# All sums of weights by the middle of the third up projection, and banks 2 and 3 of the scores in one visit for the first pair of each batch too

## The chip, the core and the metric

The kernel runs on one core of one Trainium2 chip. The metric is the device time of one execution in microseconds (us), lower is better. PE is TensorE (matmuls), DVE VectorE, ACT ScalarE, POOL GpSimd, SP SyncE, which here only starts DMAs.

## What is computed

Windowed causal attention over 8 batches, 8 heads, 576 positions and 64 dimensions per head, and then, on the attention's output taken as 4608 tokens of 512 features, a bilinear feed-forward: two up projections to 1536 features, multiplied element by element, and one down projection.

```python
scores = (q @ k.transpose(0, 1, 3, 2)) / sqrt(64) + slope[h] * (-abs(rel))    # rel = query - key
attn   = softmax(where((rel >= 0) & (rel < 128), scores, -1e9))
x      = (attn @ v).transpose(0, 2, 1, 3).reshape(8 * 576, 512)
out    = ((x @ w_a) * (x @ w_b)) @ w_out                                       # float32 in and out
```

## The kernel before, in words

**Numbers.** Almost every matmul operand is held as two float16 halves, high and low, and a product is three matmuls (high·high, high·low, low·high). `terms` (the matmul at line L820) does that for one stored form of weights against one stored form of activations: 2 blocks of the inner dimension by 3, so 6 matmuls of 128 rows by 288 columns.

**Batches and stages.** The program goes through the batches one after the other. For batch b there is an up stage ("up b" below, twelve units, one per block f of 128 hidden features) and a down stage ("down b", 48 steps of six matmuls, L916). The attention of a later batch runs in between their steps: beside up b run the third and fourth pair of heads of batch b+1, beside down b the first and second pair of batch b+2. Batch 0 is handled by code of its own (`first_attention`, `first_up`, `first_down`).

**Two kinds of up unit.** `up_plain` makes the two halves of the tokens by both projections, 4 steps of 12 matmuls: 48 matmuls. It reads the forms 0 to 3 of the block's weights. `up_fast` gets the same by seven products of sums and differences, 7 steps of 6 matmuls: 42 matmuls. It needs the activations' sums (`split_x`, on POOL, ACT and DVE, done one stage earlier) and the weights' sums (forms 3 to 6 of `wup`). Two lanes of fast units, even and odd f, are interleaved on PE. Beside its matmuls a fast unit gives ACT three reads of PSUM and a cast, DVE four adds or products and the low half of the result, and POOL one product of 128x288 elements (L875), whose result the unit's end needs.

**Sums of weights.** `sums_of_weights(f)` makes them in two steps per f, 24 steps for the twelve f. One step ("a sum" below) is five additions on POOL (L239 to L243), a cast on ACT (L244) and a subtraction on DVE (L245). Its two work tiles `wa` and `ws` come from the tag "t" with four buffers, which go round in the order of the code and which the scores use too, so POOL may have to wait at L239 or L240 until DVE has normalized an older bank of scores (L384). A sum writes over form 3, which a plain unit reads, so it can only follow the plain unit of its block. `quota` says how many sums are woven into which steps of the up and down stages 1, 2, 3; `ways` says which units of a batch are plain and which fast.

**The attention's visits.** `attention` is a generator of seven visits per pair of heads. It makes four banks of scores in PSUM: banks 0 and 1 first, later 2 and 3. A bank is some matmuls (L366), then DVE adds the bias and takes the row minimum (L370), ACT exponentiates (L371); `normalize` divides two banks at a time (ACT L383, DVE L384) into `phl`, which one DMA transposes into `pT` (L389) when all four are done. In the middle visit `pv` of the pair before runs: 42 small matmuls (L485) into two PSUM tiles `x_ps`. Score banks and `x_ps` share three PSUM buffers (`ps_at`), so the next score bank behind `pv` needs the buffer of bank 2, which is free when DVE has read bank 2. For the pairs p = 1 and p = 3 bank 3 stands behind bank 2 in the same visit; for p = 0 it stands one visit later, and p = 0 always lies in a down stage.

**What sets the order.** In the batches from 1 on PE follows the code's order exactly (`manual_schedule`); on DVE, ACT, POOL and SP a list scheduler picks the order from its own estimates at build time, and the reads of PSUM in the fast units carry a high priority. On the chip each engine's queue runs strictly in its order and waits on semaphores.

The lines that the change's two parts turn on:

```python
ways = [(every, [])] * 2 + [(every[6:], every[:6])] + [([], every)] * (B - 3)        # (plain, fast) of each batch
# per batch: ((first step, last step, sums) in the up stage, the same in the down stage)
quota = [((), ()), (((8, 48, 6),), ((0, 48, 4),)), (((0, 24, 2), (28, 66, 3)), ((0, 48, 3),)), (((0, 48, 6),), ())] + ...
# attention, middle visit of a pair (bank 2, then the product with v of the pair before)
scores(o, 2); pv(prev.p, st, prev, prev.vhl)
if two == 2 and p in (1, 3): scores(o, 3)            # otherwise one visit later
```

Of the kernel before, what the change touches and what calls it, by code (L numbers as in the profile page):

```python
# [21 lines left out]
B, H, S, D = 8, 8, 576, 64  # L22
# [24 lines left out]
def attention_then_bilinear_ffn(ctx: ExitStack, tc: tile.TileContext, qT, kT, vP, w_a, w_b, w_out, rel, slopes2, outT):  # L47
# [204 lines left out]
    def load_v(b):  # L252

        st = State()
        st.v = work.tile([P, NPAIR, VCOLS], F32, tag="v", name="v")
        sp.dma_start(st.v, vP[b])
        st.xq = work.tile([P, S], BF16, tag="xq", name="xq")
        return st
# [44 lines left out]
    def qk_squares(b, p, qk):  # L303
        o = State()
        o.b, o.p, o.qk = b, p, qk
        sums = small.tile([P, 1], F32, tag="qs", name="qs")
        hi = work.tile([P, 2, S], F16, tag="qkh", name="qkh", bufs=2)
        lo = work.tile([P, 2, S], F16, tag="qkl", name="qkl", bufs=2)
        act.activation(lo.bitcast(BF16), qk, AF.Square, accum_out=sums)

        o.both = small.tile([P, 2], BF16, tag="both", name="both")
        vec.tensor_scalar(out=o.both, in0=halves, scalar1=sums, scalar2=None, op0=ALU.mult)
        o.kh, o.kl = hi, lo
        return o
# [103 lines left out]
    def split(n, src):  # L418
        act.copy(xs[:, n, 0, :, :], src)  # L419
        vec.tensor_tensor(out=xs[:, n, 1, :, :], in0=src, in1=xs[:, n, 0, :, :], op=ALU.subtract)  # L420

    def split_x(st, plain, fast):

        b11, b12, b21, b22 = (st.v[:, k:k + 2, t:t + HT] for k in (0, 2) for t in (0, HT))
        split(0, b11)
        if plain:
            split(1, b21)
            split(2, b22)
            split(B12, b12)
        if not fast:  # L430
            return
        yield
        pool.tensor_tensor(out=b11, in0=b12, in1=b11, op=ALU.subtract)
        if not plain:
            split(2, b22)
        pool.tensor_tensor(out=b12, in0=b22, in1=b12, op=ALU.subtract)
        split(4, b11)
        pool.tensor_tensor(out=b22, in0=b22, in1=b11, op=ALU.subtract)
        yield
        if not plain:  # L440
            split(1, b21)
        split(6, b12)
        pool.tensor_tensor(out=b21, in0=b21, in1=b22, op=ALU.subtract)
        yield
        split(5, b22)
        split(3, b21)
        yield
# [194 lines left out]
    def attention():  # L642


        n = NPAIR * (B - 1)
        qks = {}

        def load(i):
            if i < n:

                qks[i] = (load_plain_qk if i < NPAIR else load_qk)(1 + i // NPAIR, i % NPAIR)

        def squares(i):
            if i >= n:
                return None
            qk = qks.pop(i)
            return qk if i < NPAIR else qk_squares(1 + i // NPAIR, i % NPAIR, qk)

        def split(o):
            if o and o.b > 1:  # L660
                split_qk(o)

        def lay_out(o):
            if o:
                before_scores(o, lay_out_qk(o) if o.b > 1 else -8.0)

        def behind():

            return tc.issue_after(last_read[0].ins) if last_read[0] else ExitStack()

        load(0)
        st, prev = load_v(1), None
        o = squares(0)
        lay_out(o)
        load(1)
        yield 0
        for i in range(n + 1):
            b, p = 1 + i // NPAIR, i % NPAIR

            two = 2 if o and o.b >= 2 else 1  # L680
            for bi in range(two if o else 0):
                scores(o, bi)
            with behind():
                nxt = squares(i + 1)
            if p == 1 and b > 1:
                st = load_v(b)
            if p == 2:
                v_scale(st)
            yield i + 1 / 7
            if o and two == 1:  # L690
                scores(o, 1)

            if p == 2:

                with tc.issue_after(first_reads[0].ins) if first_reads[0] else ExitStack():
                    late.vhl = split_v(st, late.p)
            elif prev and p != 1:
                prev.vhl = split_v(st, prev.p)
            yield i + 2 / 7
            if p == 2:  # L700
                pv(late.p, st, late, late.vhl)
                transpose_probs(prev)
                split(nxt)
            if o and p != 2:
                with behind():
                    normalize(o)
            if p != 2:
                split(nxt)
            yield i + 3 / 7
            if o:  # L710
                scores(o, 2)
            if prev and p not in (1, 2):
                pv(prev.p, st, prev, prev.vhl)
            if two == 2 and p in (1, 3):
                if p == 2:
                    with behind():
                        normalize(o)
                scores(o, 3)
            yield i + 4 / 7
            if p == 2:  # L720
                prev.vhl = split_v(st, prev.p)
                if two == 1 or p not in (1, 3):
                    with behind():
                        normalize(o)
            if o and (two == 1 or p not in (1, 3)):
                scores(o, 3)
            lay_out(nxt)
            load(i + 2)
            if p == 1:
                v_squares(st, (0, 1))  # L730
            if prev and p == 0:
                states[b - 1] = st
                assert started["down"] == b - 2
                for k, _ in enumerate(split_x(st, b - 1 <= 2, b - 1 >= 2)):
                    yield i + (4.2 + 0.2 * k) / 7
            yield i + 5 / 7
            if o:
                with behind():
                    normalize(o)
            if p == 1:  # L740
                v_squares(st, (2, 3))
            yield i + 6 / 7
            if prev and p == 0:
                hidden_scale(st)
            if p == 2:
                pv(prev.p, st, prev, prev.vhl)
            if p == 1:
                late = prev
            elif o:
                transpose_probs(o)  # L750
            prev, o = o, nxt
            yield i + 1
# [221 lines left out]


    every = list(range(NF))
    ways = [(every, [])] * 2 + [(every[6:], every[:6])] + [([], every)] * (B - 3)
    att = Pace(attention())
    spread = chain.from_iterable(sums_of_weights(f) for f in every)

    quota = [((), ()), (((8, 48, 6),), ((0, 48, 4),)), (((0, 24, 2), (28, 66, 3)), ((0, 48, 3),)), (((0, 48, 6),), ())] + [((), ())] * (B - 4)

    def first_batch():
        st = states[0]
# [60 lines left out]
```

## Time and profile before

| | |
|---|---|
| time, median of 3 runs | 1011.96 us (1011.73 to 1013.79) |
| the profiled execution | 1013.37 us, of which the traced span is 1011.6 us |
| PE busy | 969.4 us, 96% of the span |
| DVE, ACT, POOL busy | 681.8, 643.0, 305.9 us |
| PE's share of the chain of waits | 60%, DVE 12%, ACT 6%, DMA 6% |
| up 1 (all plain, 6 sums) | 81.56 us |
| down 1 (4 sums) | 42.00 us |
| up 2 (6 plain and 6 fast, 5 sums) | 80.79 us |
| down 2 (3 sums) | 41.48 us |
| up 3 (all fast, 6 sums) | 76.40 us |

How to read it: the stages' times are the distances between the first up or down matmul of one stage and that of the next, on PE's row of the timeline. A row of the stretches view gives start and end, the length, the busy time of each engine in it with the number of its instructions, the clock that TensorE was granted (1.00 is full), the share of the DMA engines and what they moved. A row of the waits view gives who waited for whom, the total in us, how often and the longest. A timeline row gives start, length, engine, line, operation, shapes and count, and in brackets the idle time before it with what ended it.

### The profile page before, as it was taken

To read this page: it belongs to the slowest core of one execution; us is meant where nothing else is said; L and a number is where in the kernel's file an instruction comes from. 1 tells how busy PE (TensorE), PEld (TensorE's weight loads), DVE (VectorE), ACT (ScalarE), POOL (GpSimd) and SP (SyncE) were. 2 spreads that over 40 slices of the span, in tenths; PEclk is the share of its full clock that TensorE was granted. 3 is DMA by queue.
4 is the path that set the end of the run, shared out by engine and by line. 5 is a ranking of instruction groups with operands and counts; after the bars stand their busy time and mean duration, and the time that the engine had idled before them with its cause. 6 is when DMAs were issued, how large, how long until landed. Compare 5 with 4: busy or idle time off the path is not lost.

```text
span 1011.6 us, 23876 instructions
## 1 busy us (share of the span) xinstructions
PE 969.4 (96%) x9327; PEld 753.2 (74%) x9327; DVE 681.8 (67%) x1884; ACT 643.0 (64%) x1668; POOL 305.9 (30%) x347
## 2 busy tenths in 40 slices
PE   8789889999999999999899999999999999999998
PEld 6557666777777777776687777777777778777776
DVE  5988999567767666787776577766677576434430
ACT  6976779666666657667666776667667766423321
POOL 3533463001445313464724022221223022221100
PEclk9889999999999999999999999999999999999999
DMA  9307643574346242464424642464423632210001
GB/s 344 132 33 276 222 124 68 113 189 87 68 96 164 67 89 57 92 161 104 87 49 107 171 89 43 95 171 101 90 63 95 168 67 43 49 36 7 1 13 36
DMA packets 148433, 102.83 MB, mean 102 GB/s; under 512 B 120032, under 2 KB 128352, under 8 KB 147296
## 3 DMA queue, kind: packets, MB, share of 16 engines
q1 hardware_dynamic: 138816, 91.77, 37.0%
q10 hardware_dynamic: 9504, 9.54, 2.9%
q8 instruction: 73, 1.20, 0.5%
q14 instruction: 40, 0.33, 0.1%
HBM read 48.33 MB, written 9.44 MB: 57 GB/s over the span
## 4 chain that ended last, share of the span: by engine, by line
PE 60%; DVE 12%; DMA 6%; ACT 6%; issue 2%; POOL 2%; SPq 0%; ACTq 0%; DVEq 0%; POOLq 0%
PE ch L820 16%; PE dn_ps L916 16%; PE p L820 12%; PE up_ps L820 11%; PE x_ps L485 3%; DMA v<-in_vP 3%; DVE phl L384 3%; PE sc_ps L366 2%; ACT t L371 2%; DVE xs L420 1%; DMA qk<-in_kT 1%; DVE t L370 1%; ACT phl L383 1%; POOL wup L135 1%; DMA qst<-qkl 1%
## 5 line engine op out<-in xcount | busy, mean ns | idle before, releaser
L820 PEld LDWEIGHTS <-wup 128*128 128x128 f16 x4212 | 407.8, 98 | 126.7 <-issue 20.5
L916 PE MATMUL dn_ps<-h,wdn 128*128 128x288 f16 x2016 | 254.0, 286 | 0.1
L820 PE MATMUL ch<-xs,wup 128*128 128x288 f16 x1584 | 228.2, 286 | 7.1 <-DVE rc L880 4.2
L916 PEld LDWEIGHTS <-wdn 128*128 128x128 f16 x2016 | 193.9, 98 | 52.1 <-issue 0.3
L820 PE MATMUL up_ps<-xs,wup 128*128 128x288 f16 x1440 | 184.8, 288 | 6.2 <-DVE rc L769 4.6
L820 PE MATMUL p<-xs,wup 128*128 128x288 f16 x1188 | 178.0, 286 | 1.1 <-ACT rc L863 1.1
L875 POOL TENSOR_TENSOR rc<-rc,row 128x288 f32<-128x288 f32 x66 | 63.8, 966 | 241.2 <-DVE row L873 223.7
L371 ACT ACTIVATE t<-t,mn 128x192 f32<-128x192 f32 (+2 forms) x252 | 107.1, 427 | 33.3 <-DVE mn L370 33.2
L384 DVE SCALAR_TENSOR_TENSOR phl<-t,rin,phl 128x192 f16<-128x192 f32 (+2 forms) x252 | 104.6, 451 | 29.1 <-ACT phl L383 28.8
L813 ACT CAST h<-rc 128x576 f16<-128x576 f32 x96 | 64.2, 669 | 64.6 <-DVE rc L880 31.9
L383 ACT ACTIVATE phl<-t,rin 128x192 f16<-128x192 f32 (+2 forms) x252 | 88.5, 426 | 16.4 <-DMA pT<-phl 10.9
L814 DVE TENSOR_TENSOR h<-rc,h 128x576 f16<-128x576 f32 x90 | 73.4, 815 | 28.8 <-ACT h L813 28.2
L370 DVE CUSTOM_DVE_ANT_0 t<-sc_ps,bias,neg 128x192 f32<-128x192 f32 (+2 forms) x216 | 73.7, 390 | 8.6 <-PE sc_ps L366 8.6
L420 DVE TENSOR_TENSOR xs<-v,xs 128x576 f16<-128x576 f32 x51 | 52.1, 1032 | 28.6 <-ACT xs L419 28.1
L857 ACT ACTIVATE row<-ch,g 128x288 f32<-128x288 f32 x66 | 32.9, 498 | 58.1 <-PE ch L820 58.1
L135 POOL TENSOR_TENSOR wup<-wup,wdn 128x512 int32<-128x512 int32 x36 | 54.6, 1537 | 44.2 <-DVE wup L133 14.1
L921 ACT ACTIVATE row<-dn_ps,oi 128x288 f32<-128x288 f32 x56 | 27.8, 496 | 60.5 <-PE dn_ps L916 59.9
L852 DVE TENSOR_TENSOR rc<-p,rc 128x288 f32<-128x288 f32 x66 | 30.0, 454 | 44.9 <-PE p L820 34.8
L239 POOL TENSOR_TENSOR wa<-wup 128x512 f32<-128x512 f16 x24 | 30.5, 1270 | 64.8 <-DVE phl L384 40.2
L348 POOL TENSOR_SCALAR bias<-rel_sb,ninv,sl_sb 128x192 f32<-128x192 f32 x24 | 18.0, 751 | 102.6 <-DVE mn L370 96.8
L880 DVE SCALAR_TENSOR_TENSOR rc<-rc,g,ch 128x288 f32<-128x288 f32 x66 | 33.6, 509 | 22.6 <-PE ch L820 22.5
L414 POOL TENSOR_TENSOR xq<-xq,sq 128x576 bf16<-128x576 bf16 x22 | 31.3, 1424 | 54.8 <-ACT sq L413 54.4
(143 smaller groups left out, 1334.0 us busy)
## 6 DMA issues: line engine op xcount, KB each, us to landing
v<-in_vP SPq DMA_DIRECT2D x8, 1280.0 KB, 6.9
out<-row ACTq DMA_DIRECT2D x60, 144.0 KB, 2.0
qk<-in_qT SPq DMA_DIRECT2D x28, 288.0 KB, 3.9
qk<-in_kT SPq DMA_DIRECT2D x28, 288.0 KB, 4.4
wdn<-in_w_a SPq DMA_DIRECT2D x12, 512.0 KB, 4.5
wdn<-in_w_b SPq DMA_DIRECT2D x12, 512.0 KB, 5.4
wdn<-in_w_out SPq DMA_DIRECT2D x12, 512.0 KB, 4.4
qst<-qkh SPq DMA_DIRECT2D x24, 144.0 KB, 2.5
```

The costliest lines, as they stand in the source:

```text
L135: pool.tensor_tensor(out=t[:, m, :], in0=t[:, m, :], in1=low[:, m, :], op=ALU.add)
L370: vec.tensor_tensor_reduce(out=t[:, c:c + w], in0=ps[:, c:c + w], in1=o.bias[:, WIN - w:WIN], scale=-0.125 if o.b == 1 else o.neg, scalar= ...
L371: act.activation(t[:, c:c + w], t[:, c:c + w], AF.Exp, bias=o.mn[:, n:n + 1], scale=-1.0, accum_out=o.sm[:, n:n + 1])
L383: act.activation(phl[:, 0, pc:pc + w], e, AF.Copy, scale=s)
L384: vec.scalar_tensor_tensor(out=phl[:, 1, pc:pc + w], in0=e, scalar=s, in1=phl[:, 0, pc:pc + w], op0=ALU.mult, op1=ALU.subtract)
L420: vec.tensor_tensor(out=xs[:, n, 1, :, :], in0=src, in1=xs[:, n, 0, :, :], op=ALU.subtract)
L813: act.copy(h[:, f, :, 0, :], hid)
L814: eng.tensor_tensor(out=h[:, f, :, 1, :], in0=hid, in1=h[:, f, :, 0, :], op=ALU.subtract)
L820: pe.matmul(ps[:, 0:HT], wup[:, a[0], a[1], wi, k, :], xs[:, b, xi, k, :], start=(first and n == 0), stop=(last and n == len(ks) - 1), ski ...
L875: pool.tensor_tensor(out=x0, in0=x0, in1=mid, op=ALU.mult)
L880: vec.scalar_tensor_tensor(out=x1, in0=x1, scalar=st.g, in1=ch, op0=ALU.mult, op1=ALU.mult)
L916: pe.matmul(ps[:, 0:HT], wdn[:, f, wi, e * P:(e + 1) * P], h[:, f, t, hi, :], start=(m == 0 and n == 0), stop=(m == NF - 1 and n == 2))
```

## The change

Two independent things. First, batch 2 loses its six plain units: all twelve are fast. So that the sums are there in time, eleven of the 24 are woven into up 1 (six before), six into down 1 (four), seven into the first 60 of the 84 steps of up 2 (five into 66), and none into down 2 and up 3 (three and six). `split_x` no longer makes the form of the activations that only plain units read (slot `B12`) for batch 2. Second, the first pair of each batch (p = 0, from batch 2 on) gets bank 3 in the middle visit, right behind `pv`, as p = 1 and p = 3 do.

```diff
-            if two == 2 and p in (1, 3):
+            if two == 2 and p in (0, 1, 3):
...
                 scores(o, 3)
             yield i + 4 / 7
             if p == 2:
                 prev.vhl = split_v(st, prev.p)
-                if two == 1 or p not in (1, 3):
+                if two == 1 or p not in (0, 1, 3):
                     with behind():
                         normalize(o)
-            if o and (two == 1 or p not in (1, 3)):
+            if o and (two == 1 or p not in (0, 1, 3)):
                 scores(o, 3)
...
-                for k, _ in enumerate(split_x(st, b - 1 <= 2, b - 1 >= 2)):
+                for k, _ in enumerate(split_x(st, b - 1 < 2, b - 1 >= 2)):
...
-    ways = [(every, [])] * 2 + [(every[6:], every[:6])] + [([], every)] * (B - 3)
+    ways = [(every, [])] * 2 + [([], every)] * (B - 2)
...
-    quota = [((), ()), (((8, 48, 6),), ((0, 48, 4),)), (((0, 24, 2), (28, 66, 3)), ((0, 48, 3),)), (((0, 48, 6),), ())] + [((), ())] * (B - 4)
+    quota = [((), ()), (((5, 48, 11),), ((0, 48, 6),)), (((0, 60, 7),), ())] + [((), ())] + [((), ())] * (B - 4)
```

PE's queue gets 72 rows shorter, 36 matmuls and their 36 loads of weights: 288 `up_ps` rows go, 144 `ch` and 108 `p` rows come.

On POOL at the start of up 2, where `wa` and `ws` are a sum's tiles and L875 is a fast unit's product, there stood before (first the end of the plain units, with L875 of the first fast unit in the last row):

```order
L239 TENSOR_TENSOR wa_5332<-wup 128x512
L348 TENSOR_SCALAR bias<-rel_sb,ninv,sl_sb 128x192
L240 TENSOR_TENSOR ws_5333<-wa_5332 128x128
L241 TENSOR_TENSOR ws_5333<-wa_5332 128x128
L242 TENSOR_TENSOR ws_5333<-ws_5333,wa_5332 128x128
L243 TENSOR_TENSOR ws_5333<-wa_5332,ws_5333 128x128
L414 TENSOR_TENSOR xq<-xq,sq 128x576
L875 TENSOR_TENSOR rc<-rc,row 128x288
```

At the start of up 2 POOL now has this:

```order
L239 TENSOR_TENSOR wa_5118<-wup 128x512
L240 TENSOR_TENSOR ws_5119<-wa_5118 128x128
L241 TENSOR_TENSOR ws_5119<-wa_5118 128x128
L875 TENSOR_TENSOR rc<-rc,row 128x288
L242 TENSOR_TENSOR ws_5119<-ws_5119,wa_5118 128x128
L243 TENSOR_TENSOR ws_5119<-wa_5118,ws_5119 128x128
L875 TENSOR_TENSOR rc<-rc,row 128x288 x2
L348 TENSOR_SCALAR bias<-rel_sb,ninv,sl_sb 128x192
L239 TENSOR_TENSOR wa_5255<-wup 128x512
L240 TENSOR_TENSOR ws_5256<-wa_5255 128x128
L241 TENSOR_TENSOR ws_5256<-wa_5255 128x128
L875 TENSOR_TENSOR rc<-rc,row 128x288
```

Sums and products of fast units now alternate in POOL's queue from the second sum of up 2 on, where before every sum up to `wa_5332` stood ahead of the stage's first L875.

On DVE in a down stage, first pair (p = 0) of a later batch, around the reads of the score banks (L370, one instruction per tile and a short one that fetches the minimum; L420 makes low halves of activations), there stood before:

```order
L370 ISA t,mn<-sc_ps,bias,neg 128x192
L370 ISA mn 128x1
L420 TENSOR_TENSOR xs<-v,xs 128x576
L370 ISA t,mn<-sc_ps,bias,neg 128x192
L370 ISA mn 128x1
L370 ISA t,mn<-sc_ps,bias,neg 128x192
L370 ISA mn 128x1
L420 TENSOR_TENSOR xs<-v,xs 128x576 x2
L379 TENSOR_SCALAR rin<-sm 128x4
L380 RECIPROCAL rin<-rin 128x4
L420 TENSOR_TENSOR xs<-v,xs 128x576
L384 SCALAR_TENSOR_TENSOR phl<-t,rin,phl 128x192 x3
```

and in the same place now:

```order
L370 ISA t,mn<-sc_ps,bias,neg 128x192
L370 ISA mn 128x1
L370 ISA t,mn<-sc_ps,bias,neg 128x192
L370 ISA mn 128x1
L370 ISA t,mn<-sc_ps,bias,neg 128x192
L370 ISA mn 128x1
L420 TENSOR_TENSOR xs<-v,xs 128x576 x2
L379 TENSOR_SCALAR rin<-sm 128x4
L380 RECIPROCAL rin<-rin 128x4
L420 TENSOR_TENSOR xs<-v,xs 128x576 x2
L384 SCALAR_TENSOR_TENSOR phl<-t,rin,phl 128x192 x4
```

Bank 3 has moved ahead of one L420, and the last of the four L384 ahead of what follows there (the reduction L500, which stood before it).

## The prediction

> **What bounds the kernel now.** I read the page's head and busy times first, then the stretches view with one stretch per stage, then PE's waits in single stages, and last the timeline at the places that the change touches.
>
> ```profile
> span 1011.6 us, 23876 instructions
> PE   969.4 (96%) x9327; PEld 753.2 (74%) x9327; DVE 681.8 (67%) x1884; ACT 643.0 (64%) x1668; POOL 305.9 (30%) x347
> PE 60%; DVE 12%; DMA 6%; ACT 6%; issue 2%; POOL 2%; SPq 0%; ACTq 0%; DVEq 0%; POOLq 0%
> 219.04 14.87 PE L820 MATMUL up_ps<-xs,wup 128*128 128x288 f16 x120
> ```
>
> PE is busy 96% of the span, and a busy PE is not yet a PE at its peak; but 120 matmuls in a row take 14.87 us, 0.1225 us each when the overlap of the last (0.16) is taken off, with nothing between them. So time in the batches is matmuls at 0.1225 us plus what PE waits. The stretches view, from up 1 to up 6, shows how much it waits (first column start and end, then the length; PE busy is the first of the busy times):
>
> ```profile
> 212.94:294.50 81.56, 80.59 (x800) 63.61 (x798) 59.30 (x174) 57.24 (x156) 24.43 (x36) 1.00 0.50 111
> 294.50:336.50 42.00, 41.17 (x408) 32.04 (x406) 30.98 (x94) 29.08 (x83) 21.09 (x23) 1.00 0.47 122
> 336.50:417.29 80.79, 77.53 (x746) 60.31 (x744) 55.48 (x147) 50.80 (x130) 28.49 (x40) 0.98 0.35 73
> 417.29:458.77 41.48, 41.20 (x409) 32.05 (x407) 30.99 (x97) 29.13 (x83) 18.49 (x22) 1.00 0.56 139
> 458.77:535.17 76.40, 71.62 (x708) 55.97 (x708) 60.48 (x157) 53.02 (x135) 35.43 (x46) 1.00 0.38 81
> 535.17:576.00 40.83, 40.83 (x408) 32.00 (x406) 24.92 (x94) 27.04 (x78) 9.12 (x7) 1.00 0.57 144
> 576.00:648.48 72.48, 71.23 (x711) 55.88 (x709) 52.62 (x151) 49.93 (x130) 16.22 (x16) 1.00 0.38 76
> ...
> 689.31:760.78 71.47, 70.90 (x711) 55.90 (x709) 51.42 (x147) 48.51 (x125) 16.14 (x16) 1.00 0.38 78
> ...
> 801.61:873.78 72.17, 71.14 (x710) 55.87 (x707) 49.40 (x140) 45.86 (x122) 15.54 (x15) 1.00 0.29 54
> ```
>
> The last three rows are up 4, 5 and 6: all fast, no sums, 72.04 us on average. Up 3 is the same work on PE with six sums beside it and takes 76.40. The only thing that it has more is the sums, so 4.36 us, 0.73 per sum, is what they cost PE there. Down 3 without sums is 40.83; down 1 (four sums) 42.00 and down 2 (three) 41.48, so 0.29 and 0.22 per sum. PE's waits in up 3 name the way:
>
> ```profile
> PE ch L820 <- DVE rc L880: 2.6, 2, 1.6
> PE p L820 <- ACT rc L863: 1.1, 1, 1.1
> PE sc_ps L366 <- DVE phl L384: 0.7, 1, 0.7
> ```
>
> and the longest of them on the timeline:
>
> ```profile
> 487.88 1.67 POOL L239 TENSOR_TENSOR wa<-wup 128x512 f32<-128x512 f16 x1
> 488.82 1.27 DVE L245 TENSOR_TENSOR wup<-ws,wup 128x512 f16<-128x512 f32 x1
> 490.01 0.50 DVE L880 SCALAR_TENSOR_TENSOR rc<-rc,g,ch 128x288 f32<-128x288 f32 x1
> 490.57 0.65 PE L820 MATMUL ch<-xs,wup 128*128 128x288 f16 x4 [1.61 <-DVE rc L880]
> L245 DVE TENSOR_TENSOR wup<-ws,wup x24: 660/692/1635, 240.9 to 506.8; 128x512 f16<-128x512 f32 x24
> ```
>
> A sum's end on DVE (L245) stands ahead of L880, the read that frees a fast unit's PSUM bank, and takes 1.27 us instead of its median 0.692 while POOL adds; PE waits 1.61 for the bank. Fast units have few banks and a tight chain; that is where a sum hurts.
>
> **Part 1, up 2 all fast.** Six units go from 48 to 42 matmuls: 36 x 0.1225 = 4.41 us that PE has less to do. Up 2 then has PE's work of up 4 to 6. By that it would be 72.04 plus seven sums. Their price lies between 0.15 (up 2 now: 80.79 - 72.04 - 4.41 leaves 4.34, of which 3.6 are shown below to be something else, so 0.75 for five sums) and 0.73 (up 3). I take 0.73, since up 3 is the nearest row: all fast, attention of the same two pairs, sums from the stage's first step. 72.04 + 7 x 0.73 = 77.1, so -3.7 us against the 80.79 of this execution.
>
> The something else stands at the start of up 2:
>
> ```profile
> 339.86 0.22 PE L366 MATMUL sc_ps<-qkh,qst 128*64 128x64 f16 x2 [1.73 <-DMA qkh<-qkh]
> 337.80:341.20 3.40, 1.51 (x28) 0.98 (x27) 2.40 (x4) 1.80 (x5) 2.93 (x5) 1.00 0.61 140
> 341.20:344.60 3.40, 3.40 (x19) 2.14 (x16) 2.39 (x15) 2.91 (x11) 1.74 (x4) 0.51 0.13 43
> ```
>
> PE waits 1.73 us (and 0.16 more) for a DMA that lays out q and k, and right after it the granted clock is 0.51 for 3.4 us, which costs another 1.7. Together 3.6. In up 3 the start wait is 0.7 and already in its 0.73 per sum. Bank 3 of down 1's first pair comes a visit earlier, so `phl` is transposed earlier and the next pair's chain with it; I take the start wait as that of up 3 and no slow stretch. If it stays whole, up 2 is some 1.2 us longer, and 1.7 more where the clock falls.
>
> [...]
>
> The new first fast unit needs all of `split_x`'s forms at once, where a plain one needed only those that are cast straight from the activations. The last form of the stage before lands at 319.26 + 0.75 = 320.0:
>
> ```profile
> 319.26 0.75 DVE L420 TENSOR_TENSOR xs<-v,xs 128x576 f16<-128x576 f32 x1
> ```
>
> and up 2 starts at 336.50: 16.5 us of cover, against two more sums of some 3.3 us POOL time in down 1 (POOL busy 21.09 of 42.00 there). Nothing; if the cover were gone, each us more would be a us of PE. The one cast and subtraction less (`B12`) lies in the same cover: nothing. Nor does a SP queue get another DMA from this part.
>
> **Part 1, elsewhere.** Up 3 without its six sums becomes a quiet stage: 72.04, -4.4 (at the least -3.9, to the slowest of the three quiet ones). Down 2 without its three: 40.83, -0.65. Down 1 gets two more sums at 0.25: +0.5 (-0.3, if the `B12` slot had cost something, to +1.5 at up 3's price). Up 1 gets five more. PE's waits there are
>
> ```profile
> PE up_ps L820 <- ACT row L806: 0.6, 1, 0.6
> PE sc_ps L366 <- DVE mn L370: 0.3, 1, 0.3
> ```
>
> 0.9 us with six sums, 0.15 each: plain units turn five banks round and read late. +0.75 (0 to 5 x 0.73 = 3.6).
>
> **Part 2, bank 3 behind `pv`.** A down stage now and a place that already has the new form:
>
> ```profile
> 545.62 0.41 DVE L370 CUSTOM_DVE_ANT_0 t<-sc_ps,bias,neg 128x192 f32<-128x192 f32 x1
> 544.63 1.63 PE L485 MATMUL x_ps<-pT,vhl 128*64 128x128 f16 x42
> 546.19 2.38 PE L916 MATMUL dn_ps<-h,wdn 128*128 128x288 f16 x18
> 548.50 0.27 PE L366 MATMUL sc_ps<-qkh,qst 128*64 128x192 f16 x2
> 549.05 0.51 SPq L335 DMA_DIRECT2D qst<-qkh  x1
> ...
> 629.51 1.63 PE L485 MATMUL x_ps<-pT,vhl 128*64 128x128 f16 x42
> 631.06 0.27 PE L366 MATMUL sc_ps<-qkh,qst 128*64 128x192 f16 x2
> 279.33 0.27 PE L366 MATMUL sc_ps<-qkh,qst 128*64 128x192 f16 x2 [0.32 <-DVE mn L370]
> ```
>
> Eighteen down matmuls are 2.21 us, and bank 3 starts 2.31 behind them: 0.10 for the change from wide to narrow matmuls. Behind `pv` it starts after 1.55, as the down matmuls do (1.56). So 0.10 goes, at six places: -0.6. What is added is a wait: bank 3 needs bank 2's buffer, whose last read ends at 545.62 + 0.41 = 546.03, and `pv` would let it start at 546.18. Cover 0.15 us; without it the price is the 0.32 of the last row, 1.9 at six places. Queued behind bank 3 on PE are the down matmuls, on DVE the low halves L420 (needed 18 us later, in the next up stage). On SP the first layout DMA (549.05) writes over what bank 3 reads, so it and the three behind it can start up to 2.3 us earlier; their number stays. I take -0.6 (to +1.3). The batches from 4 on feel this part alone.
>
> **Sum, in the profiled execution.** -3.7 (up 2), -4.4 (up 3), -0.65 (down 2), +0.5 (down 1), +0.75 (up 1), -0.6 (bank 3) = -8.1; 1013.37 - 8.1 = 1005.3. That execution is 1.4 us over the median 1011.96, about what one slow stretch of the clock costs (1.7); the three runs are 1011.73, 1011.96 and 1013.79, so I read the median as one without such a stretch. Against the median it can't be gained: -8.1 + 1.7 = -6.4, so 1005.5.
>
> **Rivals.**
> (a) The start wait and the slow stretch stay (the layout DMAs are as late as before, since down 1 has two more sums on POOL and DVE): 1005.5 + 1.2 + 1.7 = 1008.4. For it: down 1 is where more is added; against it: `phl` is done earlier. The slow stretch alone staying gives 1007.2, inside the forecast's range.
> (b) Sums hurt more in an all-fast up 2 than in up 3: each costs the 1.61 of the longest wait. Then 7 x (1.61 - 0.73) = 6.2 comes back: 1011.7, no change. Against it: only one of six did so. [...]
> (c) Slower: a sum blocks POOL. Its queue runs in order, and a sum waits for a buffer of tag "t":
>
> ```profile
> 370.18 1.26 POOL L239 TENSOR_TENSOR wa<-wup 128x512 f32<-128x512 f16 x1 [26.86 <-DVE phl L384]
> POOL wa L239 <- DVE phl L384: 2.7, 1, 2.7
> POOL ws L240 <- DVE phl L384: 2.8, 3, 2.2
> ```
>
> The first row stood in up 2 beside plain units, which need nothing of POOL. In the all-fast stage L875 stands behind it. The fast units' results go through three buffers, so two units of 7 x 6 x 0.1225 = 5.1 us can run on; a wait of more than some 10 us stops PE, and more than 10 + 6.4 + 2 = 18 makes the kernel slower; at 26.86 it would be 1005.5 + 16.9 = 1022. Against it: in up 3 such waits were at most 2.7 us (the two rows of its waits), and the order puts three L875 ahead of the next such wait.
>
> **Chances.** The forecast with its own range 1002.5 to 1007.5: 0.58. Better than that (sums at 0.15): 0.08. (a): 0.17. (b): 0.10. (c): 0.07. Faster by over 0.2% (below 1009.9; 0.2%, 2 us, is about what a measurement of this kernel can tell from no change): forecast, better, (a) and a part of (b), 0.84; within 0.2%: 0.09; slower: 0.07. The range leaves out (c), most of (b) and the tail of the better: 1002.0 to 1009.8.
>
> **What would show it.** Up 2 at 77 us and up 3 at 72; PE's waits in up 2 on L880 and L863; down 2 at 40.8; in the down stages bank 3 directly behind `pv` with no wait, 40.7 each. I am wrong if up 2's L875 or L239 shows waits over 10 us, if up 3 stays at 76 (then its cost was not the sums), or if the six down stages get longer.

## The result, and the profile after

The changed kernel takes 1022.18 us (median of four runs, 1017.95 to 1029.40) against 1011.85 beside it: 1.0113 of the time before, interval 1.0092 to 1.0134 (the two medians alone give 1.0102). It is slower; forecast was 1005.5. The profiled execution is the quickest of the four, 1017.95 us. First the page's head (span, busy times), then the stretches view of up 1 to up 6 and, last, of one piece of up 1:

```profile
span 1016.1 us, 23832 instructions
PE 964.2 (95%) x9291; PEld 749.7 (74%) x9291; DVE 686.6 (68%) x1895; ACT 643.1 (63%) x1673; POOL 316.5 (31%) x353
```

```profile
211.97:298.54 86.57, 82.22 (x800) 64.39 (x798) 69.30 (x178) 59.46 (x160) 42.66 (x60) 0.98 0.46 103
298.54:341.85 43.31, 41.12 (x409) 32.08 (x407) 32.41 (x99) 30.42 (x86) 29.12 (x33) 1.00 0.47 119
341.85:419.20 77.35, 71.67 (x711) 55.95 (x709) 61.77 (x158) 53.63 (x136) 40.82 (x55) 1.00 0.38 81
419.20:459.93 40.73, 40.73 (x408) 32.10 (x406) 25.12 (x92) 25.80 (x75) 9.19 (x7) 1.00 0.49 122
459.93:534.40 74.47, 71.31 (x711) 55.99 (x709) 52.76 (x152) 50.95 (x134) 15.86 (x16) 1.00 0.44 88
534.40:575.13 40.73, 40.73 (x408) 32.10 (x406) 25.42 (x94) 26.74 (x78) 9.19 (x7) 1.00 0.53 132
575.13:648.79 73.66, 71.32 (x711) 55.99 (x709) 52.49 (x151) 50.02 (x130) 16.15 (x16) 1.00 0.40 86
689.53:763.83 74.30, 71.32 (x711) 55.99 (x708) 52.73 (x152) 50.19 (x130) 16.15 (x16) 1.00 0.41 86
804.57:878.27 73.70, 71.23 (x709) 55.98 (x707) 49.72 (x140) 46.62 (x124) 15.55 (x15) 1.00 0.30 61
281.54:284.95 3.41, 2.95 (x18) 1.87 (x19) 1.75 (x9) 2.64 (x10) 1.19 (x2) 0.50 0.64 164
```

PE is busy 5.2 us less (36 fewer matmuls are 4.4), and yet the span is 4.5 us longer. By stage, the profiled execution against that of the kernel before:

| | forecast | measured |
|---|---|---|
| up to the start of up 1 | 0 | -1.0 |
| up 1 (11 sums, 6 before) | +0.75 | +5.0 |
| down 1 (6 sums, 4 before) | +0.5, less 0.1 | +1.3 |
| up 2 (all fast) | -3.7 | -3.4 |
| down 2 (no sums) | -0.65, less 0.1 | -0.7 |
| up 3 (no sums) | -4.4 | -1.9 |
| down 3, 4, 5 | -0.1 each | -0.1 each |
| up 4, 5, 6 | 0 | +1.2, +2.8, +1.5 |
| sum | -8.1 | +4.5 |

PE's waits name two places, the start of the up stages and the end of up 1:

```profile
PE sc_ps L366 <- DVE mn L370: 5.2, 2, 3.7
PE sc_ps L366 <- DMA qkh<-qkh: 4.1, 3, 1.4
PE sc_ps L366 <- DVE phl L384: 2.2, 1, 2.2
PE sc_ps L366 <- DMA qkl<-qkl: 1.9, 4, 1.2
```

Before, the first took 0.5 us, the second stood only at the start of up 2, the third (at the start of up 3) took 0.7 and the fourth 0.4 us in all. The timeline of down 3 to the start of up 4 shows where they come from. L326 casts q and k of the next pair to their high half, L327 makes the low half, L335 to L338 are the four DMAs that lay them out, L265 is a square of v for the next batch:

```profile
568.35 0.74 ACT L265 ACTIVATE vsq<-v 128x640 bf16<-128x640 f32 x1 [2.93 <-DMA v<-in_vP]
569.09 1.24 ACT L326 ACTIVATE qkh<-qk,own 128x1152 f16<-128x1152 f32 x1
570.35 0.47 SPq L335 DMA_DIRECT2D qst<-qkh  x1
570.36 1.42 DVE L327 SCALAR_TENSOR_TENSOR qkl<-qk,own,qkh 128x1152 f16<-128x1152 f32 x1 [4.31 <-ACT qkh L326]
573.12 0.56 SPq L337 DMA_DIRECT2D qkh<-qkh  x1
574.43 0.46 SPq L338 DMA_DIRECT2D qkl<-qkl  x1
577.46 0.22 PE L366 MATMUL sc_ps<-qkh,qst 128*64 128x64 f16 x2 [1.43 <-DMA qkh<-qkh]
```

The same place in the kernel before:

```profile
566.13 1.24 ACT L326 ACTIVATE qkh<-qk,own 128x1152 f16<-128x1152 f32 x1
567.40 0.47 SPq L335 DMA_DIRECT2D qst<-qkh  x1
570.25 0.74 ACT L265 ACTIVATE vsq<-v 128x640 bf16<-128x640 f32 x1 [2.88 <-DMA v<-in_vP]
570.74 0.47 SPq L337 DMA_DIRECT2D qkh<-qkh  x1
576.83 0.22 PE L366 MATMUL sc_ps<-qkh,qst 128*64 128x64 f16 x2
```

ACT has exchanged two neighbours. Before, the cast ran first and L265 waited 2.88 us for v behind it, holding up nobody. Now L265 stands first, the cast waits behind it, DVE waits 4.31 us for the cast, and L337, the third DMA of the layout, is issued 2.4 us later, though up 4 now starts 0.9 us earlier; PE pays 1.43 us. Nothing in the code asks for that: the list scheduler, which orders ACT, chose otherwise once bank 3 had moved. In the kernel before it had made the same choice in down 0, 1 and 2, which is why up 2 started with a wait of 1.73 us there.

The other place, the end of up 1, after (the sums' L245, the scale of q and k from L107 on, bank 2's first read L370; PE's first L366 is bank 2, its second bank 3):

```profile
274.21 0.93 DVE L245 TENSOR_TENSOR wup<-ws,wup 128x512 f16<-128x512 f32 x1
276.06 0.27 PE L366 MATMUL sc_ps<-qkh,qst 128*64 128x192 f16 x2
276.14 1.10 DVE L245 TENSOR_TENSOR wup<-ws,wup 128x512 f16<-128x512 f32 x1 [1.00 <-ACT wup L244]
277.58 0.15 DVE L107 TENSOR_SCALAR cl<-qtot 128x2 f32<-128x2 f32 x1
279.85 1.42 DVE L327 SCALAR_TENSOR_TENSOR qkl<-qk,own,qkh 128x1152 f16<-128x1152 f32 x1 [0.21 <-ACT qkh L326]
281.19 0.41 DVE L370 CUSTOM_DVE_ANT_0 t<-sc_ps,bias,neg 128x192 f32<-128x192 f32 x1
282.00 0.37 PE L366 MATMUL sc_ps<-qkh,qst 128*64 128x192 f16 x2 [3.72 <-DVE mn L370]
```

and before:

```profile
272.16 1.44 DVE L245 TENSOR_TENSOR wup<-ws,wup 128x512 f16<-128x512 f32 x1
274.68 0.15 DVE L107 TENSOR_SCALAR cl<-qtot 128x2 f32<-128x2 f32 x1
276.76 1.42 DVE L327 SCALAR_TENSOR_TENSOR qkl<-qk,own,qkh 128x1152 f16<-128x1152 f32 x1 [0.43 <-ACT qkh L326]
278.52 0.41 DVE L370 CUSTOM_DVE_ANT_0 t<-sc_ps,bias,neg 128x192 f32<-128x192 f32 x1
```

Bank 2 lies ready from 276.6 us on, but DVE reads it at 281.19, since two sums (before one) and then the whole scale of q and k stand ahead. Bank 3 needs bank 2's buffer: 3.72 us of PE, and the clock is 0.50 for 3.41 us from 281.54 on, in which PE is busy 2.95: another 1.5. DVE's groups in up 1 show why it is so far behind, before and then after (count, total in us, mean in ns):

```profile
L384 DVE SCALAR_TENSOR_TENSOR phl<-t,rin,phl 128x192 f16<-128x192 f32 (+2 forms) x27 | 10.8, 447 | 0.6 <-ACT phl L383 0.4
L833 DVE SCALAR_TENSOR_TENSOR rc<-rc,g,up_ps 128x288 f32<-128x288 f32 x23 | 11.6, 508 | 1.5 <-PE up_ps L820 0.9 <-PE qtot L320 0.6
L245 DVE TENSOR_TENSOR wup<-ws,wup 128x512 f16<-128x512 f32 x6 | 5.0, 832 | 1.0 <-ACT wup L244 1.0
```

```profile
L384 DVE SCALAR_TENSOR_TENSOR phl<-t,rin,phl 128x192 f16<-128x192 f32 (+2 forms) x27 | 14.8, 594 | 0.6 <-ACT phl L383 0.4
L833 DVE SCALAR_TENSOR_TENSOR rc<-rc,g,up_ps 128x288 f32<-128x288 f32 x23 | 11.5, 504 | 1.3 <-PE up_ps L820 1.3
L245 DVE TENSOR_TENSOR wup<-ws,wup 128x512 f16<-128x512 f32 x11 | 9.5, 860 | 4.5 <-ACT wup L244 4.4
```

Five more sums add 4.5 us of L245 to DVE, but its busy time in up 1 goes from 59.30 to 69.30 us, 2.0 per sum: L384, which reads two operands from SBUF, grows from 447 to 594 ns while POOL is busy 42.66 us instead of 24.43. L833, which reads PSUM, stays (508 and 504 ns). In up 1 of the changed kernel an L384 of 128x192 takes 412 to 419 ns without a POOL instruction beside it and up to 1312 with one.

### The profile page after: what moved, and what is told of

It reads as the page before. It is cut to its first block, busy times and chain, and to the rows that moved or that the text cites. A ratio compares the mean times of both kernels' runs of the same rounds, so it can differ in the third digit from the quotient of the medians.

```text
span 1016.1 us, 23832 instructions
## 1 busy us (share of the span) xinstructions
PE 964.2 (95%) x9291; PEld 749.7 (74%) x9291; DVE 686.6 (68%) x1895; ACT 643.1 (63%) x1673; POOL 316.5 (31%) x353
## 4 chain that ended last, share of the span: by engine, by line
PE 53%; DMA 6%; DVE 6%; ACT 3%; issue 1%; SPq 0%; POOL 0%; ACTq 0%; DVEq 0%; POOLq 0%
PE ch L820 18%; PE dn_ps L916 17%; PE p L820 13%; DMA v<-in_vP 3%; PE x_ps L485 3%; PE sc_ps L366 2%; DVE phl L384 2%; DMA qk<-in_kT 2%; ACT t L371 1%; DMA qst<-qkl 1%; DVE t L370 1%; ACT qkh L326 1%; DVE qkl L327 1%; DVE h L814 1%; DVE rc L880 1%
## 5 line engine op out<-in xcount | busy, mean ns | idle before, releaser
L820 PE MATMUL ch<-xs,wup 128*128 128x288 f16 x1728 | 248.8, 286 | 8.3 <-DVE rc L880 6.0
L820 PE MATMUL p<-xs,wup 128*128 128x288 f16 x1296 | 194.2, 286 | 0.0
L820 PE MATMUL up_ps<-xs,wup 128*128 128x288 f16 x1152 | 147.9, 287 | 6.1 <-DVE rc L769 4.6
L875 POOL TENSOR_TENSOR rc<-rc,row 128x288 f32<-128x288 f32 x72 | 69.2, 961 | 264.6 <-DVE row L873 253.9
L384 DVE SCALAR_TENSOR_TENSOR phl<-t,rin,phl 128x192 f16<-128x192 f32 (+2 forms) x252 | 105.5, 453 | 33.1 <-ACT phl L383 32.9
L383 ACT ACTIVATE phl<-t,rin 128x192 f16<-128x192 f32 (+2 forms) x252 | 88.4, 426 | 15.7 <-DMA pT<-phl 11.5
L814 DVE TENSOR_TENSOR h<-rc,h 128x576 f16<-128x576 f32 x90 | 73.6, 818 | 24.1 <-ACT h L813 23.3
L370 DVE CUSTOM_DVE_ANT_0 t<-sc_ps,bias,neg 128x192 f32<-128x192 f32 (+2 forms) x216 | 73.8, 389 | 11.1 <-PE sc_ps L366 11.1
L857 ACT ACTIVATE row<-ch,g 128x288 f32<-128x288 f32 x72 | 35.9, 498 | 65.0 <-PE ch L820 65.0
L420 DVE TENSOR_TENSOR xs<-v,xs 128x576 f16<-128x576 f32 x50 | 49.4, 1000 | 24.8 <-ACT xs L419 24.3
L880 DVE SCALAR_TENSOR_TENSOR rc<-rc,g,ch 128x288 f32<-128x288 f32 x72 | 36.7, 509 | 25.1 <-PE ch L820 25.1
L366 PEld LDWEIGHTS <-qst 128*64 128x64 f16 x864 | 31.2, 110 | 28.2 <-issue 19.6
L366 PE MATMUL sc_ps<-qkh,qst 128*64 128x192 f16 (+2 forms) x432 | 40.1, 246 | 11.6 <-DVE mn L370 5.2
```

The source lines that it names most:

```text
L366: pe.matmul(ps[64 * e:64 * e + 64, c:c + w], o.qs[:, e, qq], ks[:, e, kk], start=not last, stop=last)
L370: vec.tensor_tensor_reduce(out=t[:, c:c + w], in0=ps[:, c:c + w], in1=o.bias[:, WIN - w:WIN], scale=-0.125 if o.b == 1 else o.neg, scalar= ...
L383: act.activation(phl[:, 0, pc:pc + w], e, AF.Copy, scale=s)
L384: vec.scalar_tensor_tensor(out=phl[:, 1, pc:pc + w], in0=e, scalar=s, in1=phl[:, 0, pc:pc + w], op0=ALU.mult, op1=ALU.subtract)
L814: eng.tensor_tensor(out=h[:, f, :, 1, :], in0=hid, in1=h[:, f, :, 0, :], op=ALU.subtract)
L820: pe.matmul(ps[:, 0:HT], wup[:, a[0], a[1], wi, k, :], xs[:, b, xi, k, :], start=(first and n == 0), stop=(last and n == len(ks) - 1), ski ...
```

## The experiments

Two theories for the up stages. A: the order on ACT is the whole loss of part 2. Rival: bank 3's new place itself, through its buffer and DVE's order. For part 1: D, a sum costs by where it stands on DVE; rival, by the number of sums. Further theories come with e10 (E, a sum costs by its subtraction L245 on DVE; rival F, by POOL) and e13 (G, a sum's price goes by the stage it stands in). Where a kernel has two more code lines, L882, L835 and L816 are L880, L833 and L814. The kernel before ran beside each group: 1012.8 us beside e1 to e4, 1012.4 beside e5 to e8, 1012.2 beside e9 to e12, 1011.9 beside e13 to e15.

**e1, part 1 alone.** `p in (0, 1, 3)` goes back to `p in (1, 3)` in its three places.

> Part 1 alone (the sums moved, up 2 all fast), bank 3 where it was. Theory A, order on ACT: the waits at the start of up 4, 5 and 6 in the changed kernel come from part 2 alone, which puts a square of v that waits for its DMA (L265) ahead of the cast of q and k (L326) on ACT. Here L326 stands first again in down 3 to 5: up 4 to 6 are 72.0 us each as before (the changed kernel 73.9), no PE wait on the DMA of qkh there; up 1 keeps its 5 us more, up 2 its 3.4 less, up 3 2 to 4 less: 1009 to 1013 us. Theory B, the moved sums are what costs: as slow as the changed kernel, 1018 us or more. Theory C, all of the loss is bank 3's: 1005 us with up 1 at 82.

1014.54 us, ratio 1.0011 (1.0001 to 1.0020); the profiled execution 1010.77. Up 4 to 6 are 71.9, 72.3 and 71.6 without a wait on the layout, up 1 87.6, up 2 77.9, up 3 72.0. So the waits of up 4 to 6 are not part 1's, up 3 is at the 72.0 that was forecast, and up 1 keeps its loss. (In this build the cast stands ahead of the square in down 2 too, which it did not before; e6 shows what that is worth in up 3.) The median is above the 1009 to 1013 expected: part 1, forecast at -7.5 of the -8.1, gains nothing.

**e2, part 2 alone.** Only the three conditions change.

> Part 2 alone (banks 2 and 3 of the first pair in one visit), the sums where they were. Theory A, order on ACT: L265 stands ahead of L326 in all of down 0 to 5; PE waits some 1.4 us for the DMA of qkh at the start of up 4, 5 and 6, which are 1.2 to 2.8 us longer each; down stages 0.1 shorter each: span 1011.6 + 5.5 - 0.6 = 1016.5 or so, 1015 to 1022 us by how many half-clock stretches follow the waits. Theory B, the moved sums cost it: 1011.3 us, no waits on qkh in up 4 to 6.

1021.04 us, ratio 1.0084 (1.0071 to 1.0097). Up 4 and 6 in the stretches view, and the start of up 4:

```profile
572.76:649.24 76.48, 72.83 (x711) 56.76 (x709) 52.98 (x152) 51.66 (x136) 16.20 (x17) 0.98 0.42 85
804.62:881.19 76.57, 72.75 (x710) 56.77 (x708) 50.10 (x142) 48.08 (x129) 15.53 (x15) 0.98 0.33 64
576.43 0.22 PE L366 MATMUL sc_ps<-qkh,qst 128*64 128x64 f16 x2 [2.78 <-DMA qkh<-qkh]
```

Part 2 alone, forecast at -0.6, costs 8.2 us, nearly what both cost together. Here the wait is 2.78 us, and a stretch at half clock follows it in both stages (mean clock 0.98).

**e3, part 2 with ACT's order mended.**

```diff
-        act.activation(hi, qk, AF.Copy, scale=own)
+        o.cast = act.activation(hi, qk, AF.Copy, scale=own)
...
             if p == 1:
-                v_squares(st, (0, 1))
+                with tc.issue_after(nxt.cast.ins) if b > 1 else ExitStack():
+                    v_squares(st, (0, 1))          # the same for (2, 3)
```

> Part 2 alone, with the four squares of v (L265) held behind the cast of q and k (L326) on ACT. Theory A, order on ACT: the start waits of up 4 to 6 are gone (72.0 each), and those which the kernel before has at the start of up 2 (1.73 + 0.16 us and a half-clock stretch of 1.7) and up 3 (0.7) shrink too: 1011.9 - 0.6 - (1.7 to 3.6) = 1007.5 to 1010 us. Rival, bank 3 itself costs the time (its PSUM buffer, DVE's order): the start waits stay although ACT's order is mended, 1015 to 1022 us as part 2 alone.

1009.36 us, ratio 0.9969 (0.9958 to 0.9981), and its runs lie within 1.0 us of each other. Up 4 and up 5:

```profile
570.76:643.31 72.55, 71.21 (x710) 55.88 (x708) 52.60 (x151) 50.03 (x130) 16.15 (x16) 1.00 0.38 75
684.06:755.52 71.46, 70.90 (x710) 55.89 (x708) 52.04 (x150) 48.99 (x127) 16.15 (x16) 1.00 0.37 80
```

Bank 3 is where part 2 puts it and the waits are gone. The order of two neighbours on ACT, mended here in down 0 to 2 as well, is 11.7 us between e2 and this.

**e4, both parts with ACT's order mended.**

> The changed kernel with the four squares of v (L265) held behind the cast of q and k (L326) on ACT. Theory A, order on ACT: up 4 to 6 come back to 72.0 (5.5 us less in all), the start wait of up 3 (2.2) goes, up 1 keeps 3 to 5 us of its loss: 1016.1 + 1.85 - 5.5 - 2.2 = 1010.3 us, 1007 to 1012, and runs agree better with each other. Rival: the sums on DVE and POOL delay the layout, whatever ACT's order: the waits on qkh stay, 1016 to 1022 us.

1013.44 us, ratio 1.0009 (0.9996 to 1.0022): some 9 us come back, but no gain over the kernel before is left. The median is above the range, and the runs agree no better than before (1010.2 to 1018.6): the waits of up 1 (3.6 us) and up 2 (1.9 and 2.0) are still there, and the mean clock of up 1 is 0.98 (in the profiled executions a stretch at half clock followed 13 of 13 gaps above 2.5 us and 3 of 18 from 1.7 to 2.5). Up 1 is 86.6 us, down 1 43.1, up 2 77.0, up 3 72.6. Against e3, which lacks only part 1, it is 4.1 us slower, and up 2 takes 77.0 us in both: the matmuls saved there pay for the sums and no more.

**e5, the bad order without the change.** The kernel before; in the visit p = 1 the first square is made before the cast, and the cast held behind it (lines move by two: L310, L859, L368 are L309, L857, L366).

```diff
-                split(nxt)
+                split(nxt, v_squares(st, (0,)) if p == 1 and b > 1 else None)    # cast issued behind that square
```

> The kernel before, with nothing of the change, but with the first square of v (L265) put ahead of the cast of q and k on ACT in every down stage. Theory A, the order on ACT is the whole loss of part 2: PE waits 1.4 to 2.8 us for the DMA of qkh at the start of up 4, 5 and 6 too, these stages are 73.5 to 76.5 us instead of 71.5 to 72.5: 1016 to 1021 us, as part 2 alone (1021.0). Rival, bank 3's move itself makes the wait: no change, 1012.8.

1026.11 us, ratio 1.0137 (1.0124 to 1.0151), more than theory A's 1016 to 1021. Up 4, 5 and 6 are 77.5, 76.0 and 75.4. So the order alone costs as much, with nothing of the change, but mostly not by the wait that A had: at the start of up 4 PE waits only 0.2 and 0.9 us for the layout. Most of the loss is a second step, here in up 4:

```profile
581.48 1.16 ACT L310 ACTIVATE qkl<-qk 128x1152 bf16<-128x1152 f32 x1 [2.67 <-DMA qk<-in_kT]
585.20 0.90 PE L822 MATMUL ch<-xs,wup 128*128 128x288 f16 x6 [2.81 <-ACT row L859]
```

The late cast also makes the load of the next q and k late (its second half is issued at 576.57, in the kernel before at 571.90), and the next ACT instruction that waits for that load holds up the read of a PSUM bank (L859).

**e6, the mended order without the change.**

> The kernel before with only the cast of q and k held ahead of the squares of v on ACT in the down stages. Theory A: the start wait of up 2 (1.9 us) and the half-clock stretch behind it (1.7) go, up 3 gives 1 us: 1009.5 to 1011 us; then part 2 itself is worth the rest down to the 1009.4 of part 2 with this order, 0.1 per down stage, some 0.6. Rival, the order helps only with bank 3 moved: 1012.8.

1010.34 us, ratio 0.9976 (0.9967 to 0.9985). Up 2 starts without the 1.73 us and without the slow stretch and is 77.66 us instead of 80.79; up 3 starts without its 0.7 and 0.2 and is 75.55 instead of 76.40. Between this and e3 the ratios do not separate part 2's own worth; in the profiled executions down 1 is 41.1 instead of 42.0, down 2 41.0 instead of 41.35 and down 3 to 5 40.74 instead of 40.83 each, 1.6 us in all.

**e7, no sums around the last layout of up 1.** e4 with `(5, 30, 7), (40, 48, 4)` for `(5, 48, 11)`.

> The changed kernel with the order on ACT mended, and up 1's eleven sums given at steps 5 to 30 (seven) and 40 to 48 (four), so that none stands on DVE directly ahead of the scale of q and k (L107 to L327) of the pair laid out in up 1; 1013.4 us without this. Theory D, the place on DVE costs up 1 its 5 us (bank 2's reads come late, bank 3 waits 3.6 us, and a half-clock stretch of 1.7 follows): up 1 82 to 83.5 us instead of 86.6, no wait of bank 3 over 0.5 us, 1008.5 to 1010 us in all. Rival, the number of sums costs 1 us each wherever they stand: up 1 stays at 86, 1013 us.

1011.75 us, ratio 0.9997 (0.9985 to 1.0010). Up 1 is 82.9 us and bank 3's wait 1.4 (D had 0.5 at most), so the place counts there; but down 1 is 46.4:

```profile
303.90 1.14 PE L918 MATMUL dn_ps<-h,wdn 128*128 128x288 f16 x8 [2.42 <-DVE h L816]
```

The four sums at the end of up 1 delay the last hidden blocks (L816), down 1 waits 2.42 us for them, and a slow stretch follows (mean clock of down 1 0.96). Up 2 has another one (0.98) and is 79.4. Against e4 the 3.7 us gained in up 1 are given back in the two stages behind it (3.3 and 2.4); the intervals of the two ratios overlap.

**e8, six sums in up 1, twelve in up 2.** e4 with `(8, 48, 6)`, `(0, 48, 6)`, `(0, 60, 12)`.

> The changed kernel with the order on ACT mended, six sums in up 1 as in the kernel before, six in down 1, twelve in up 2 (up to its step 60 of 84). By the prices seen (up 2 with seven sums 77.0, without 72.0, 0.7 each): up 1 81.5, up 2 80.5, 1013.4 - 5.1 + 3.5 = 1011.8 us. Theory D, only the place of a sum on DVE counts: up 2 stays near 77 to 78, 1008.5 to 1009.5 us.

1015.54 us, ratio 1.0033 (1.0021 to 1.0045), worse than either theory. Up 1 is 81.3, as forecast, but up 2:

```profile
336.61:423.75 87.14, 75.26 (x711) 57.69 (x709) 70.83 (x163) 56.37 (x140) 57.86 (x80) 0.96 0.32 69
PE ch L822 <- DVE rc L882: 7.3, 3, 2.9
```

Five more sums than in e4 cost 10.1 us there, two slow stretches among them (mean clock 0.96). Beside fast units the price rises with the number.

**e9, all eleven sums of up 1 early.** e4 with `(5, 30, 11)`.

> The changed kernel with the order on ACT mended (1013.4 us) and all eleven sums of up 1 given at its steps 5 to 30, none at its end. Theory D, the place on DVE: up 1 82 to 83.5 us (bank 3's wait of 3.6 and the half-clock stretch behind it gone), down 1 no longer than 43.1, since no sum holds back the last h of up 1: 1008 to 1010 us. Rival, the number of sums sets it: up 1 86 again, 1013 us.

1012.59 us, ratio 1.0008 (0.9999 to 1.0017). Up 1 is 88.6 with bank 3's wait of 3.7 again, though no sum stands directly ahead of the scale of q and k. DVE starts that scale (L107) 5.2 us after PE started its input (L320 at 275.35), in the kernel before 0.7. Theory D in this form falls: packed together, the sums leave DVE behind all the same. Down 1 is 41.3.

**e10, L245 on POOL.** e4 with `pool.tensor_tensor` for `vec.tensor_tensor` at L245.

> The changed kernel with the order on ACT mended, the last subtraction of each sum (L245, 128x512) on POOL instead of DVE, sums at their places. Theory E, a sum costs PE by L245, which stands on DVE ahead of a read that frees a PSUM bank: up 2's waits on L882 (1.85 and 1.96 us) go, up 2 73.5 to 75 us instead of 77.0, up 1 82 to 84 instead of 86.6: 1004 to 1008 us. Rival F, POOL: each sum holds POOL some 1.5 us longer (L239 of the same shape takes 1.2 to 1.7), DVE's operations beside it stretch and fast units' L875 queue behind it: up 2 stays at 77 or more, 1012 to 1018 us.

1011.27 us, ratio 0.9992 (0.9983 to 1.0001). Up 1 is 85.9 with a wait of 3.5, up 2 78.6 with waits on L882 of up to 1.9: theory E falls, and the 1012 to 1018 of its rival F are not met either. There is not one L245 on DVE, and its L384 in up 1 is as slow as with them (610 ns, e4 595):

```profile
L384 DVE SCALAR_TENSOR_TENSOR phl<-t,rin,phl 128x192 f16<-128x192 f32 (+2 forms) x27 | 15.2, 610 | 0.9 <-ACT phl L383 0.8
L816 DVE TENSOR_TENSOR h<-rc,h 128x576 f16<-128x576 f32 x11 | 11.2, 1020 | 6.0 <-ACT h L815 5.8
```

What a sum costs DVE is not only the instruction that DVE runs for it.

**e11, e9 and e10 together.**

> Both of the last two: the sums of up 1 at steps 5 to 30 and the subtraction on POOL, order on ACT mended. Theories D and E together: up 1 82, up 2 74, down 1 42: 1003 to 1007 us. If POOL becomes the limit where sums stand densely (11 x some 5.5 us in 45 us of up 1 are more than fit), they slide into down 1 and delay it: 1010 us or more.

1015.32 us, ratio 1.0032 (1.0020 to 1.0045). Up 1 is 91.1 us, with half the clock for 6.83 us of it. The sums did not slide into down 1 as the last sentence of the expectation had it: down 1 is 41.0. POOL is busy 57.0 us of up 1; that it is the limit there is not shown.

**e12, e3 with L245 on POOL.**

> Part 2 alone with the order on ACT mended (1009.4 us) and the subtraction L245 on POOL, the sums where the kernel before has them. Theory E: up 3 (75.3 with six sums) comes to 73 to 74, up 2 (77.0) to 76, 1006 to 1008 us. Rival F: no gain or a loss, 1009.4 to 1013 us.

1008.50 us, ratio 0.9967 (0.9955 to 0.9979): not to be told from e3. Up 3 is 75.0 (e3 75.3), so not theory E's 73 to 74; up 2 is 75.9 (e3 77.0), as E had it.

**e13, eleven sums in up 1, all else as in e3.** `(8, 48, 6)` becomes `(5, 48, 11)` and up 3's `(0, 48, 6)` becomes `(0, 48, 1)`. Blocks 6 and 7 are summed here before their plain units of up 2 have read them, so these units compute with other numbers; the instructions are the same in kind and number.

> Part 2 with the order on ACT mended (1009.4 us), up 2 half plain as before, but five of up 3's six sums moved to up 1, which has eleven. Theory G: up 1 goes from 81.4 to 86 or 87 (bank 3's wait of 3.6 us and a half-clock stretch), up 3 from 75.3 to 72.5: 1011 to 1012 us. Rival, up 1's loss comes with the all-fast up 2 behind it: up 1 82, up 3 72.5: 1007 us.

1010.63 us, ratio 0.9988 (0.9977 to 0.9999). Up 1 and up 3:

```profile
212.59:299.61 87.02, 82.25 (x799) 64.30 (x797) 70.24 (x182) 59.86 (x161) 42.72 (x60) 0.98 0.46 104
459.67:531.71 72.04, 71.24 (x710) 55.96 (x708) 53.20 (x151) 50.07 (x130) 19.03 (x21) 1.00 0.39 83
```

Up 1's loss is its own: 81.4 to 87.0 with five more sums, whatever up 2 is. Up 3 gives 3.2 back.

**e14, sums spread 7, 5, 6, 4, 2; e15, the same with nine fast and three plain units in up 2** (`every[9:], every[:9]`, up 2's sums `(0, 58, 6)`).

> Part 2 with the order on ACT mended (1009.4 us), up 2 half plain as before, sums spread 7, 5, 6, 4, 2 over up 1, down 1, up 2, down 2, up 3 (before 6, 4, 5, 3, 6). Theory G: up 3 with two sums instead of six gains 2 to 2.5 us, the four others one more each cost 0.2 to 0.3: 1007 to 1008 us. Rival, six is the limit in up 1 and the seventh already brings bank 3's wait: 1010 us or more.

> As the last, but nine fast units and three plain ones in up 2 instead of six and six: 18 matmuls less, 18 x 0.1225 = 2.2 us. Theory G: up 2's six sums now stand mostly beside fast units and take 1 to 3 us back: 1006 to 1008.5 us, about as the last. Rival, fast units cost nothing more: 1005 us.

e14: 1008.57 us, ratio 0.9965 (0.9951 to 0.9978), not to be told from e3. Up 1 is 81.6, so seven sums still fit; up 3 with two sums is 74.0, only 1.3 below its six, and up 2 1.9 longer, so a price per sum, theory G's too, is too simple.
e15: 1006.95 us, ratio 0.9956 (0.9944 to 0.9969), the lowest median of all, 4.9 us below the kernel before beside it and 15 below the changed one; its interval overlaps e14's. Up 2 is 79.5, no shorter than e14's 78.9: the 2.2 us of matmuls saved there went into waits, and most of the 1.9 us that its span has less stand in stages that are the same in both (up 4 and up 6).

## Why the prediction was wrong, by its own steps

**"`phl` is transposed earlier and the next pair's chain with it."** This step failed, and with it the sign. It followed the chain over PE, DVE and SP and left out ACT, on which the cast L326 heads that chain. I took bank 3's move to change nothing there, but the new build puts L265 ahead of L326 in down 3 to 5 as well. The layout right behind bank 3 did start earlier, as forecast (L335 at 546.01 against 549.05); the next pair's starts later (570.35 against 567.40). In the sum this is part 2's -0.6 (to +1.3), which alone measured +8.2. Shown by e2 (the move alone, 1021.0), e3 (the move with the cast ahead, 1009.4) and e5 (the square ahead without the move, 1026.1, in part by a longer way). Rival (a) had the start wait of up 2 staying, for another reason, and no rival had it arise in stages where it was not.

**Up 2, -3.7, and down 2, -0.65:** right, -3.4 and -0.7. In the forecast's own terms the sums' rise from 0.75 to 5.1 us eats the 4.4 of matmuls, and the gain is the start wait and the slow stretch. So it came: the wait fell from 1.9 to 1.2 us, the stretch is gone, and in e3 and e4, which have neither, up 2 is 77.0 with six plain units and with none.

**Up 3, -4.4:** over-sized. The step took the sums for the only thing that up 3 had more than up 4 to 6, but in down 2 the square already stood ahead of the cast; with that order mended and all six sums (e6) up 3 is 75.55, so the sums were worth 3.5 us, 0.6 each. Of this the changed kernel shows 1.9, since it waits 2.2 us at the start of up 3: the square in down 2 now waits 3.91 us for v, before 1.17. With ACT's order mended it is 72.6, so that loss is the first step's again.

**Up 1, +0.75 (0 to 3.6):** the mis-sized term. It measured +5.0, with ACT's order mended (e4) and with up 2 half plain (e13) too. 0.15 per sum was an average over six sums that fitted; I did not ask whether DVE's queue had room for eleven. Nor did the step look at what a sum takes of DVE: five more take 10.0 us, not only the 4.5 of their L245.

**Down 1, +0.5, and bank 3's cover of 0.15 us:** the forecast bounded a lost cover by 0.32 us. In down 1, where six sums stand on DVE, the cover is gone and bank 3 waits 1.5 (its row above, 5.2 us in two waits, is this and the 3.7 of up 1); in down 2 to 5 it holds, with no wait. Per place the 0.10 was right: 40.83 to 40.74.

**The slow stretch.** The forecast took the stretch at up 2's start as going with the wait. The runs side with it: in e6 and e3 the wait went and the stretch with it (mean clock of up 2 1.00 in both, 0.98 in the kernel before). PE was not idle all the time ahead of it: in the 3.40 us before the stretch in the kernel before it was busy for 1.51, while in up 1 of the changed kernel it was idle for all of the 3.26 us before (278.28 to 281.54).

**Rival (b)** did not come true: with seven sums up 2 is 5.3 us over the 72.04, 0.76 per sum. With twelve (e8) it is 15.1 over, 1.26 per sum, on the way to the 1.61 that (b) had.

**Rival (c)** (a sum blocking POOL ahead of L875) played no part: in up 2 L239 has no long wait any more, POOL's longest is 6.6 us (L875 for DVE), and PE's longest are on L880, none on L875's results.

**The medians.** Between the profiled executions (1013.37 and 1017.95) lie 4.6 us, between the medians 10.3. The other three runs of the changed kernel have mean clocks of 0.980 to 0.985, the profiled one 0.990. One stretch of 3.41 us at half clock takes 0.0017 off the mean; 0.005 to 0.010 are three to six of them, by that estimate 5 to 10 us, and the three runs are 3.4 to 11.5 us slower. They were not traced, so where the stretches lie in them is not shown, and the table by stage, of the quickest of the four, accounts for 4.5 us alone.

What stays open: why the scheduler exchanged the two, and what a sum costs at each place. The numbers say that it depends on what stands around it on DVE and POOL, not on its count alone.

## What to carry to other kernels

Where a scheduler orders an engine, a change in one place can exchange two instructions in another; before forecasting, look on every engine of the chain that you count on, in the new build, for an instruction that waits for a load and now stands ahead of one that others wait for. A price per piece, averaged over pieces that fitted, says nothing of the next ones: look at how far the reader's queue lags behind. And a saving of matmuls is worth only what the work that must move with it leaves over: here, with the order mended, every kernel with up 2 all fast (e4, e7 to e11, ratios 0.9992 to 1.0033) is slower than e3, which has it half plain (0.9969).

## What the runs showed of the hardware

**Gaps and the clock.** In the seventeen profiled executions I counted the gaps of PE over 1.2 us from 140 us on, and whether a stretch at half clock began within 9 us. Below 1.7 us: none of 53. 1.7 to 2.0 us: 2 of 15 (a third, in e11, is followed by a gap of 2.87, to which I put its stretch). 2.0 to 2.5: 1 of 3. Above 2.5: 13 of 13. The stretches begin 2 to 5 us behind the gap's start and last 3.41 us (one 6.83). So in these kernels a wait of over 2.5 us cost PE up to 1.7 us more than itself (an estimate, half of the 3.41), and one of 1.2 to 1.7 itself alone.

**POOL and DVE.** Five more sums take 18.2 us more of POOL in up 1. Of DVE's operations with two SBUF operands the mean of L384 grows by a third (447 to 594 ns) and that of L814 by a sixth (803 to 931), while L327 and L284 stay (1418 to 1415, 882 to 878). In up 1 of the changed kernel an L384 of 128x192 without a POOL instruction beside it takes 412 to 419 ns and the longest with one 1312; all ten that took over 420 had one. Not every operation beside POOL is longer: an L327 with POOL beside it for 1.15 us stays at 1405 ns. L833, which reads PSUM, does not change (508 to 504 ns). An L113 of 128x2, with one operand, took 1158 ns instead of 128 to 169 beside one L239 and ended with it (at 245.53 and 245.50 us). Moving L245 to POOL takes the 9.5 us of the eleven L245 from DVE in up 1, and about half of it comes back: DVE is busy 65.3 us with e10 and 70.1 with e4, and the means of L816, L284 and L327 go from 918, 878 and 1488 to 1020, 1157 and 1758 ns.
